# The state update of a linear-attention kernel: one full-array product per head pair, or one 32-column product per head half

## The chip, the core and the metric

The kernel runs on one core of a Trainium2 chip. A core has five engines that run side by side and meet through semaphores: TensorE (PE) for matmuls, VectorE (DVE), ScalarE (ACT), GpSimd (POOL), and SyncE (SP), which here only issues transfers. TensorE reads its operands from SBUF, the 128-partition working memory, and writes to PSUM, the accumulator memory. Weights are loaded by an operation of its own, shown as PEld. The metric is the device time of one execution in microseconds.

## The reference: what is computed

Two blocks follow each other. The first is a linear attention with a decaying state (RWKV-5): 4 batches, 8 heads, 768 positions, head dimension 48. For each position t of a head,

```
y_t   = r_t . (state + (u * k_t) v_t^T)
state = w * state + k_t v_t^T          (w: one decay per head and row, constant in time)
```

The results of all heads, joined to rows of 384, go into a feed-forward block: `silu(x @ w_gate) * (x @ w_val) @ w_out` with inner size 1536, for 3072 rows. All data are fp32; the weights come as 64-bit floats and are rounded to fp32 on the chip.

## The kernel before

**Units.** The sequence is cut into 6 chunks of 128 positions. A unit is one chunk of one batch, all 8 heads; unit i is chunk i // 4 of batch i % 4, so that the state that unit i leaves is read by unit i + 4. There are 24 units. Within a chunk the recurrence is a masked product: `scores` (line 377) makes k times r for each head, a masked copy (line 388, VectorE) puts the upper triangle into the tile `At`, and `outputs` (line 393) multiplies v by `At` and adds the state's share, `Z` times `rT`. The state left by a chunk is `w^128 * (state + khat^T v)`, where `khat` is k scaled so that each position's decay is right.

**Heads in pairs.** Heads 2a and 2a+1 share the partitions: head e of the pair has rows 64e to 64e+47, with rows 48 to 63 empty. `Z[b]` has 128 partitions, 4 pairs and 96 columns, 48 for each head of the pair; only the two blocks in which row head and column head agree may hold anything, the other two must be zero, since y sums over 112 rows of both heads.

**y in column groups.** `outputs` writes 32 partitions of PSUM at a time: four matmuls with 32 weight columns each go to four column groups of TensorE (line 413), and the loop order `for n: for q in range(4)` puts the four groups next to each other.

**The update.** `update(i)` (line 419) takes one matmul per pair over all 112 rows and 96 columns of the pair (line 426), so the products of one head's k with the other head's v are made too. The table `wL` (built once, line 756, from w^128 and the 0/1 table `own`) is zero for them: for the first chunk VectorE multiplies the PSUM result by it into Z (line 437); later VectorE adds the PSUM result to Z (line 439) and GpSimd multiplies Z by the table (line 440). The last chunk has no update, which leaves 20 updates.

**Order of the work.** Every engine runs its queue in program order, and the program is laid out by hand in a loop over steps s (line 803). In step s the unit s+1 is scaled, unit s is turned, scores of unit s-1 and y and update of unit s-2 are made. In between, `gaps(s, n)` hands out pieces of the feed-forward block from the list `todo`, mostly `four` (line 593, sums of products in a scheme that saves multiplications; its matmuls are line 628) and `project` (line 501; line 522). Up to step 11 the gaps also hold the rounding of the weights (`round_act`, `round_dve`, `round_pool`: lines 170 to 207), whose chunks of 768 KB arrive by transfers. From step 12 (`LATE`) y of unit s-2 stands directly behind the scores of unit s-1; before, it stands after the gap 2. The update stands after gap 3 in all of these steps. The first four units are written out ahead of the loop, and their updates too.

**The PSUM ring.** Scores (two tiles), y and update take their tiles from one ring of four, `ps_a`.

**The start.** `make_identity` on GpSimd is followed by 18 matmuls with the identity [...] (line 256, `warm`), then the transposes of unit 0 (line 341), the decay tables on VectorE (lines 272 to 288, `pw`, `pv`), and `own_product`, the u term, on GpSimd (lines 223, 224).

Of the kernel before, what the change touches and what calls it, by code (L numbers as in the profile page):

```python
# [9 lines left out]
FP32 = mybir.dt.float32  # L10
# [3 lines left out]
ALU = mybir.AluOpType  # L14
AX = mybir.AxisListType
P = 128
# [6 lines left out]
def fast(  # L23
# [25 lines left out]
    B, H, S, D = r.shape  # L49
    D2 = 2 * D  # L50
    VW = 2 * D + 16
    HP = H // 2
    R2 = 64 + D
# [5 lines left out]
    cst = ctx.enter_context(tc.tile_pool(name="cst", bufs=1))  # L59
# [4 lines left out]
    ps_a = ctx.enter_context(tc.tile_pool(name="ps_a", bufs=4, space=bass.MemoryType.PSUM))  # L64
# [3 lines left out]
    dve, pool, act, pe, sp = nc.vector, nc.gpsimd, nc.scalar, nc.tensor, nc.sync  # L68
# [3 lines left out]
    ub = cst.tile([P, H, D], FP32, name="ub")  # L72
    kscale = cst.tile([P, H, D], FP32, name="kscale")
    rscale = cst.tile([P, H, D], FP32, name="rscale")
    own = cst.tile([P, 2], FP32, name="own")
    wL = cst.tile([P, HP, 2, D], FP32, name="wL")
    w128 = cst.tile([P, HP], FP32, name="w128")
    bad = cst.tile([P, HP], FP32, name="bad")
    held = cst.tile([P, HP], FP32, name="held")
# [9 lines left out]
    Z = [cst.tile([P, HP, D2], FP32, name=f"Z{b}") for b in range(B)]  # L89
# [29 lines left out]
    def load_v(i):  # L119
        c, b = divmod(i, B)  # L120
        rows = slice(P * c, P * (c + 1))
        for e in range(2):
            sp.dma_start(
                out=v_ld[i % 4][:, :, 64 * e : 64 * e + D],
                in_=v[b, :, rows, :].rearrange("(a e) t d -> e t a d", e=2)[e],
            )
# [82 lines left out]
    def round_weights():  # L209
        if done["act"] > done["pool"]:  # L210
            round_pool()
        round_act()
# [3 lines left out]
    def own_product(i):  # L216
        kl, rl = raw(i)
        if i == 1:

            rk = At[1][:, 0:3, :].rearrange("p x t -> p (x t)").rearrange("p (h d) -> p h d", h=H)  # L220
        else:
            rk = one.tile([P, H, D], FP32, name="rk", tag="rk")[:]
        pool.tensor_mul(rk, rl, kl)
        pool.tensor_mul(rk, rk, ub[:])
        rks[i] = rk

    def own_sum(i):
        dus[i] = three.tile([P, H], FP32, name="du", tag="du")
        dve.tensor_reduce(dus[i][:], rks.pop(i), axis=AX.X, op=ALU.add)
# [4 lines left out]
        dve.memset(t[:, :, D:64], 0.0)  # L234
    dve.memset(hats[:, 0:6, :, D:64], 0.0)
    dve.memset(wcol[:], 1.0)
    for e in range(2):
        sp.dma_start(out=wcol[64 * e : 64 * e + D, :], in_=w.rearrange("(a e) d -> e d a", e=2)[e])
    load(0)
    sp.dma_start(  # L240
        out=ub[:].rearrange("p h d -> p (h d)"),
        in_=bass.AP(tensor=u.tensor, offset=u.offset, ap=[[0, P], [1, H * D]]),
# [9 lines left out]
    def warm(n):  # L252

        ps = ps_f.tile([P, 2, 2 * P], FP32, name="warm", tag="gv")
        for _ in range(n):
            pe.matmul(ps[:, 0, 0:P], ident[:], ident[:], start=True, stop=True)

    warm(18)

    pool.memset(own[:], 1.0)  # L260
    for step, base in ((-64, 0), (64, D - 1)):
        pool.affine_select(
            out=own[:], in_=own[:], compare_op=ALU.is_ge, fill=0.0,
            base=base, pattern=[[step, 2]], channel_multiplier=1 if step < 0 else -1,
        )

    pool.memset(mask[:], 1.0)
    pool.affine_select(
        out=mask[:], in_=mask[:], compare_op=ALU.is_gt, fill=0.0,
        base=0, pattern=[[1, P]], channel_multiplier=-1,  # L270
# [23 lines left out]
    def at(i, a):  # L294

        return HP - 1 - a if i >= BLOCKS and i % 2 == 0 else a
# [14 lines left out]
    def scale(i):  # L311
        scale_k(i)
        scale_r(i)
# [18 lines left out]
    def pair(t, a):  # L332
        return t[:, 2 * a : 2 * a + 2, :].rearrange("p e d -> p (e d)")
# [59 lines left out]
    def outputs(i):  # L393

        c, b = divmod(i, B)
        A, vl, z = At[i % 2], v_ld[i % 4], Z[b]
        rT = turned.pop(i)
        ps = ps_a.tile([P, CC, P], FP32, name="y_ps", tag="a")  # L400
        cols = [[] for _ in range(4)]
        for m in range(4 * CC):
            (cc, q), (a, s) = divmod(m, 4), divmod(m, 3)
            each = [(z[0:R2, a, 32 * s : 32 * s + 32], rT[0:R2, at(i, a), :])] if c > 0 else []
            if s < 2:
                each.append((vl[:, a, 32 * s : 32 * s + 32], A[:, 2 * a, :]))
            if s > 0:
                each.append((vl[:, a, 32 * s + 16 : 32 * s + 48], A[:, 2 * a + 1, :]))
            cols[q] += [(cc, x, n == 0, n == len(each) - 1) for n, x in enumerate(each)]
        for n in range(len(cols[0])):  # L410
            for q in range(4):
                cc, x, start, stop = cols[q][n]
                pe.matmul(  # L413
                    ps[32 * q : 32 * q + 32, cc, :], *x,
                    start=start, stop=stop, skip_group_check=True,
                )
        act.copy(xT[:, i % NX, :, :], ps[:])

    def update(i):
        c, b = divmod(i, B)  # L420
        if c == NCH - 1:
            return
        kh, vl, z = khat[i % 4], v_ld[i % 4], Z[b]
        ps = ps_a.tile([P, HP, D2], FP32, name="u_ps", tag="a")
        for a in range(HP):
            pe.matmul(  # L426
                ps[0:R2, a, :].rearrange("p (e d) -> p e d", e=2),
                pair(kh, a)[:, 0:R2],
                bass.AP(
                    tensor=vl.tensor, offset=vl[:, a, 0:1].offset,  # L430
                    ap=[list(vl[:].ap[0]), [64, 2], [1, D]],
                ),
                start=True, stop=True, skip_group_check=True,
            )
        w = wL[0:R2].rearrange("p a e d -> p a (e d)")
        if c == 0:
            dve.tensor_mul(z[0:R2], ps[0:R2], w)
        else:
            dve.tensor_add(z[0:R2], ps[0:R2], z[0:R2])
            pool.tensor_mul(z[0:R2], z[0:R2], w)  # L440


    hT = {}
# [30 lines left out]
    def weight_sum():  # L474

        n = len(summed)
        o = (wt[1][:], w12, wt[0][:], wt[2][:])[n]
        a, b = ((w22, w12), (w12, w11), (w22, w12), (w21, wt[0][:]))[n]
        pool.tensor_sub(o, a, b)
        summed.append(n)  # L480
# [198 lines left out]
    def feed(n, pops=1):  # L679
        for _ in range(n):  # L680
            ready = [k for k, (need, _) in enumerate(todo) if need <= done["pool"] + len(summed)]
            if ready:
                todo.pop(ready[0])[1]()
            for _ in range(min(pops, len(small))):
                small.popleft()()
# [18 lines left out]
    def gaps(s, n):  # L704

        if s not in EARLY:
            if n == 0:
                share[0] = min(-(-len(todo) // (4 - (s - 9) % 4)), 14)
            feed(share[0] // 5 + (n < share[0] % 5))
            return  # L710
        for what in EARLY[s][n]:
            if what == "R":
                if done["pool"] < NW:
                    round_weights()
                elif len(summed) < 4:
                    weight_sum()
            else:
                feed(1, 3)
# [20 lines left out]
    while small:  # L739
# [13 lines left out]
    outputs(1)  # L753
    round_pool()
    dve.tensor_copy(w128[:].unsqueeze(2), pw[:, :, 0:1])
    dve.tensor_mul(
        wL[:], w128[:].unsqueeze(2).unsqueeze(3).to_broadcast([P, HP, 2, D]),
        own[:].unsqueeze(1).unsqueeze(3).to_broadcast([P, HP, 2, D]),
    )

    dve.tensor_tensor(bad[:], held[:], wcol[:], ALU.not_equal)
    dve.tensor_reduce(badc[:], bad[:], axis=AX.X, op=ALU.add)
# [8 lines left out]
    turn(2)  # L771
    own_product(3)
    update(0)
    update(1)
    own_sum(2)
    diagonal(2)
# [26 lines left out]
    for s in range(4, N + 2):  # L803
        if 4 < s < N:
            own_sum(s)
        if s + 1 < N:
            scale(s + 1)
            own_product(s + 1)
            load_v(s + 1)
            if s + 3 < N:  # L810
                load(s + 3)
        if s < BLOCKS:
            turn(s)
        gaps(s, 0)
        if 4 <= s - 1 < N:
            while small:
                small.popleft()()
            scores(s - 1)
            if s >= LATE:
                outputs(s - 2)  # L820
            gaps(s, 1)
        if BLOCKS <= s < N:
            turn_blocks(s)
        if BLOCKS <= s + 1 < N:
            move_blocks(s + 1)
        gaps(s, 2)
        if s - 2 >= 4 and (s < LATE or s > N):
            outputs(s - 2)
        if s >= 5 and s % 2:
            queue((s - 3) // 2)  # L830
        if s < N:
            diagonal(s)
        if s - 2 >= 4:
            gaps(s, 3)
            update(s - 2)
        gaps(s, 4)
        if s == 12:
            n_ps = ps_a.tile([P, HP, P], FP32, name="n_ps", tag="a")
            pe.matmul(n_ps[0:1, 0, 0:1], badc[:], ones[:], start=True, stop=True)
            act.copy(outside, n_ps[0:1, 0, 0:1])  # L840
# [417 lines left out]
```

## Time and profile before

The median of three runs is 640.49 us (639.94 to 641.51). The profiled execution spans 638.3 us.

| what | number |
|---|---|
| TensorE busy | 624.0 us, 98% of the span |
| VectorE, GpSimd, ScalarE busy | 367.4, 299.1, 242.0 us |
| share of TensorE in the chain that ended last | 85% |
| of it, the update's matmuls (L426) | 2% |
| update: matmul records, mean | 160, 267 ns |
| y: matmul records, mean | 768 of 279 ns and 480 of 276 ns |
| VectorE, add of the update (L439) | 16 of 555 ns |
| GpSimd, product with the table (L440) | 16 of 1056 ns |
| building the table (L756) | 1 of 2186 ns |

How to read it: matmuls overlap each other, so the mean duration of a record is not what it costs; the distance from one start to the next is. Each fp32 matmul of the program appears as two matmul records and two weight loads. A shape such as 128*112 128x96 means 128 rows, 112 weight columns, and 96 streamed columns. The chain of waits goes back from the last instruction to what released it; it says on which engine the end depends at each time.

### The profile page before, as it was taken

The numbers are of one execution on the slowest core, as the hardware profiler recorded it, in microseconds if no ns is written. First come the engines' busy times: TensorE is split into PE (matmuls) and PEld (weight loads), VectorE is DVE, ScalarE is ACT, GpSimd is POOL, SyncE is SP. The second block draws the span as 40 slices with busy tenths as digits, with TensorE's granted clock in tenths as the row PEclk, the third lists the DMA queues.
The fourth block names the chain that finished last, engine by engine and source line by source line (L and its number), as shares of the span: only waits on it lengthen the run. The fifth ranks groups of instructions, "written<-read, shape, count | busy, mean of one in ns | idle before, by whom it ended". The sixth has DMA issues, their size and how long they took to land.

```text
span 638.3 us, 11992 instructions
## 1 busy us (share of the span) xinstructions
PE 624.0 (98%) x4570; PEld 561.6 (88%) x4570; DVE 367.4 (58%) x729; ACT 242.0 (38%) x655; POOL 299.1 (47%) x330
## 2 busy tenths in 40 slices
PE   8889999999999999999999999999999999999996
PEld 8678888899888889988899988889988889988896
DVE  7859998455356565366558255666255545355460
ACT  3558776421343421244431234442243320234310
POOL 5868877934837431754534734631432311444110
PEclk9989999999999999999999999999999999999998
DMA  8969873233322113212221402021100000000001
GB/s 197 263 161 232 223 213 89 40 65 73 79 48 37 33 26 71 66 32 52 45 47 31 109 5 46 16 40 27 51 1 2 1 1 26 26 1 1 2 2 53
DMA packets 138003, 40.40 MB, mean 63 GB/s; under 512 B 128592, under 2 KB 131792, under 8 KB 137936
## 3 DMA queue, kind: packets, MB, share of 16 engines
q1 hardware_dynamic: 134480, 34.82, 24.8%
q10 hardware_dynamic: 3456, 4.72, 2.1%
q8 instruction: 38, 0.62, 0.4%
q14 instruction: 29, 0.24, 0.1%
HBM read 28.51 MB, written 4.72 MB: 52 GB/s over the span
## 4 chain that ended last, share of the span: by engine, by line
PE 85%; DVE 8%; ACT 3%; POOL 1%; issue 1%; DMA 0%; SPq 0%; DVEq 0%; ACTq 0%
PE c_b L628 24%; PE c_a L628 20%; PE o_f L522 13%; PE o_a L522 8%; PE o_b L522 6%; PE y_ps L413 5%; PE gv L451 4%; PE s_ps L383 3%; PE u_ps L426 2%; ACT At L320 1%; DVE wg L196 1%; DVE At L388 1%; DVE wv L196 1%; ACT w_mag L178 1%; DVE wv L197 1%
## 5 line engine op out<-in xcount | busy, mean ns | idle before, releaser
L612 POOL TENSOR_TENSOR hT<-hT,u 128x256 f32<-128x256 f32 x60 | 47.5, 792 | 161.2 <-DVE hT L611 134.2
L635 ACT COPY u<-c_a 128x256 f32<-128x256 f32 x120 | 44.5, 371 | 86.9 <-PE c_a L628 85.6
L628 PE MATMUL c_a<-t,wv 128*128 128x256 f32 x240 | 72.2, 382 | 0.1
L628 PE MATMUL c_b<-xT,wg 128*128 128x256 f32 x240 | 71.7, 380 | 0.0
L608 ACT ACTIVATE sg<-hT 128x256 f32<-128x256 f32 x120 | 50.0, 416 | 54.2 <-DVE hT L637 35.5
L320 ACT ACTIVATE At<-ident,du 128x128 f32<-128x128 f32 x180 | 63.0, 398 | 12.5 <-DVE o_sb L536 7.8
L628 PE MATMUL c_b<-xT,s 128*128 128x256 f32 x240 | 61.6, 379 | 0.0
L642 DVE TENSOR_TENSOR u<-u,c_b 128x256 f32<-128x256 f32 x60 | 25.1, 418 | 62.1 <-PE c_b L628 55.1
L628 PEld LDWEIGHTS c_b<-xT,s 128*128 128x128 f32 x240 | 45.3, 190 | 6.6 <-DVE u L642 0.2
L628 PEld LDWEIGHTS c_a<-t,wv 128*128 128x128 f32 x240 | 44.7, 190 | 7.0 <-ACT u L635 1.1
L628 PEld LDWEIGHTS c_b<-xT,wg 128*128 128x128 f32 x240 | 45.2, 190 | 6.2 <-issue 0.4
L588 POOL TENSOR_TENSOR s<-wv,wg 128x256 f32<-128x256 f32 x24 | 17.8, 741 | 69.8 <-PE o_f L522 55.3
L637 DVE TENSOR_TENSOR hT<-p,c_b 128x256 f32<-128x256 f32 x60 | 25.2, 419 | 43.5 <-PE c_b L628 40.0
L388 DVE COPY_PREDICATED At<-mask,s_ps 128x512 f32<-128x512 int32 x48 | 32.8, 739 | 18.1 <-PE s_ps L383 10.8
L413 PE MATMUL y_ps<-At,v_ld 128*32 128x128 f32 x768 | 36.1, 279 | 4.7 <-DVE At L388 4.7
L451 PE MATMUL gv<-xT,wg 128*128 128x256 f32 x144 | 36.8, 391 | 0.0
L644 DVE TENSOR_TENSOR hT<-u,c_b 128x256 f32<-128x256 f32 x60 | 25.2, 421 | 19.4 <-PE c_b L628 19.2
L413 PEld LDWEIGHTS y_ps<-At,v_ld 128*32 128x32 f32 x768 | 30.9, 112 | 6.1 <-DVE At L388 5.7
L628 PE MATMUL c_b<-t,s 128*128 128x256 f32 x120 | 36.2, 383 | 0.0
L640 DVE TENSOR_TENSOR hT<-hT,c_a 128x256 f32<-128x256 f32 x60 | 25.3, 421 | 18.9 <-PE c_a L628 17.5
L628 PE MATMUL c_b<-xT,wv 128*128 128x256 f32 x120 | 35.9, 381 | 0.0
L628 PE MATMUL c_a<-xT,wg 128*128 128x256 f32 x120 | 35.8, 380 | 0.0
(139 smaller groups left out, 1411.7 us busy)
## 6 DMA issues: line engine op xcount, KB each, us to landing
hats<-hats SPq DMA_DIRECT2D x192, 32.0 KB, 1.9
w_bits<-in_moe_w_gate_dram SPq DMA_DIRECT2D x6, 768.0 KB, 5.9
v_ld<-in_v_dram SPq DMA_DIRECT2D x48, 96.0 KB, 3.0
w_bits<-in_moe_w_val_dram SPq DMA_DIRECT2D x6, 768.0 KB, 5.8
w_bits<-in_moe_w_out_dram SPq DMA_DIRECT2D x6, 768.0 KB, 5.1
out_dram<-o_sb ACTq DMA_DIRECT2D x24, 192.0 KB, 1.9
k_ld<-in_k_dram SPq DMA_DIRECT2D x22, 192.0 KB, 2.8
r_ld<-in_r_dram SPq DMA_DIRECT2D x22, 192.0 KB, 3.7
```

What stands on the lines that cost most here:

```text
L320: lambda h=h: act.activation(At[i % 2][:, h, :], ident[:], AF.Identity, scale=du[:, h : h + 1])
L388: dve.copy_predicated(At[i % 2][:].rearrange("p (a e) t -> p a e t", e=2)[:, :, e], mask[:].bitcast(INT32).unsqueeze(1).to_broadcast([P, H ...
L413: pe.matmul(ps[32 * q : 32 * q + 32, cc, :], *x, start=start, stop=stop, skip_group_check=True,)
L451: pe.matmul(gv[:, o, :].rearrange("p (i t) -> p i t", i=2), wt[:, c, P * f : P * (f + 1)], xT[:, 2 * g % NX : 2 * g % NX + 2, c, :], start ...
L522: pe.matmul(ps, lhs[:, f, :], rhs[:, f, :], start=(f == 0 and n in (0, 1, 4)), stop=(f == FH - 1), skip_group_check=True,)
L608: act.activation(x[what, f][:], h[j], AF.Sigmoid)
L612: pool.tensor_mul(h[1], h[1], x.pop(("u3", f))[:])
L628: pe.matmul(ps.rearrange("p (i t) -> p i t", i=2), lhs, rhs, start=first, stop=what not in ("p2", "p5", "p4", "p3"), skip_group_check=True,)
L635: act.copy(x[nm, f][:], ps)
L637: dve.tensor_add(h[0], x.pop(("p1", f))[:], ps)
L640: dve.tensor_mul(h[0], h[0], ps)
L644: dve.tensor_add(h[1], x.pop(("u2", f))[:], ps)
```

## The change

Each head's share of the state is made by itself. Instead of one product of 112 by 96 per pair there are four products of 32 weight columns and 48 streamed columns, one for each half (32 rows) of each head, each in its own column group of TensorE, as in y. The products of one head with the other are no longer made, so the table that zeroes them, `wL`, and `own` go away. In their place Z is set to zero once at the start, on GpSimd, and the sums and products touch only the blocks of a head: two operations per update, 48 partitions by 192 elements each, with w^128 broadcast along the columns. Last, the update moves from behind gap 3 to directly behind y of the same unit, where the array is already set to 32-column groups.

```diff
-    own = cst.tile([P, 2], FP32, name="own")
-    wL = cst.tile([P, HP, 2, D], FP32, name="wL")
...
     dve.memset(wcol[:], 1.0)
+    for z in Z:
+        pool.memset(z[:], 0.0)
...
     warm(18)
-
-    pool.memset(own[:], 1.0)
-    for step, base in ((-64, 0), (64, D - 1)):
-        pool.affine_select(
-            out=own[:], in_=own[:], compare_op=ALU.is_ge, fill=0.0,
-            base=base, pattern=[[step, 2]], channel_multiplier=1 if step < 0 else -1,
-        )
...
-        ps = ps_a.tile([P, HP, D2], FP32, name="u_ps", tag="a")
+        ps = ps_a.tile([P, HP, D], FP32, name="u_ps", tag="a")
         for a in range(HP):
-            pe.matmul(
-                ps[0:R2, a, :].rearrange("p (e d) -> p e d", e=2),
-                pair(kh, a)[:, 0:R2],
-                bass.AP(
-                    tensor=vl.tensor, offset=vl[:, a, 0:1].offset,
-                    ap=[list(vl[:].ap[0]), [64, 2], [1, D]],
-                ),
-                start=True, stop=True, skip_group_check=True,
-            )
-        w = wL[0:R2].rearrange("p a e d -> p a (e d)")
-        if c == 0:
-            dve.tensor_mul(z[0:R2], ps[0:R2], w)
-        else:
-            dve.tensor_add(z[0:R2], ps[0:R2], z[0:R2])
-            pool.tensor_mul(z[0:R2], z[0:R2], w)
+            for q in range(4):
+                e, half = divmod(q, 2)
+                pe.matmul(
+                    ps[32 * q : 32 * q + 32, a, :], kh[:, 2 * a + e, 32 * half : 32 * half + 32],
+                    vl[:, a, 64 * e : 64 * e + D],
+                    start=True, stop=True, skip_group_check=True,
+                )
+        for e in range(2):
+            rows = slice(64 * e, 64 * e + D)
+            ze = z[rows, :, D * e : D * e + D]
+            w = w128[rows].unsqueeze(2).to_broadcast([D, HP, D])
+            if c == 0:
+                dve.tensor_mul(ze, ps[rows], w)
+            else:
+                dve.tensor_add(ze, ps[rows], ze)
+                pool.tensor_mul(ze, ze, w)
...
     dve.tensor_copy(w128[:].unsqueeze(2), pw[:, :, 0:1])
-    dve.tensor_mul(
-        wL[:], w128[:].unsqueeze(2).unsqueeze(3).to_broadcast([P, HP, 2, D]),
-        own[:].unsqueeze(1).unsqueeze(3).to_broadcast([P, HP, 2, D]),
-    )
...
             if s >= LATE:
                 outputs(s - 2)
+                update(s - 2)
             gaps(s, 1)
...
         if s - 2 >= 4 and (s < LATE or s > N):
             outputs(s - 2)
+            update(s - 2)
...
             gaps(s, 3)
-            update(s - 2)
         gaps(s, 4)
```

## The prediction

> **What bounds the kernel now.** I read the busy shares first, then the slices, then the chain of waits in order of time, then the single matmuls around one update.
>
> ```profile
> PE 624.0 (98%) x4570; PEld 561.6 (88%) x4570; DVE 367.4 (58%) x729; ACT 242.0 (38%) x655; POOL 299.1 (47%) x330
> PE   8889999999999999999999999999999999999996
> ```
>
> TensorE is the bound by share, but the first slices show gaps, so the stages must be parted. The chain in order of time does that:
>
> ```profile
> 21.56 2.19 DVE wL L756
> 23.75 0.89 DVE bad L761
> ...
> 37.55 1.55 PE u_ps L426 x8
> ...
> 98.80 0.48 DVE Z L439
> ...
> 99.33 1.16 PE s_ps L383 x14
> ```
>
> Up to 99.3 us the chain runs mostly over VectorE and ScalarE (rounding of the weights, masks, decay tables), with TensorE on it only from about 36 to 47 us. From 99.3 us to the end it is TensorE almost alone. Busy time by stretch says the same: from 100 to 600 us TensorE is busy for 499.89 of 500 us, VectorE for 269.66, GpSimd for 224.01. So after 99.3 us a TensorE nanosecond saved is a nanosecond of the end, and before it only VectorE's and ScalarE's row counts, with the exception from 36 to 47.
>
> One update in the full stage (start, duration):
>
> ```profile
> 295.90 0.59 PE L628 MATMUL c_b<-xT,wg 128*128 128x256 f32 x2
> 296.34 0.94 PE L426 MATMUL u_ps<-v_ld,hats 128*112 128x96 f32 x8
> 297.11 0.62 PE L628 MATMUL c_a<-t,wv 128*128 128x256 f32 x2
> ```
>
> Each fp32 matmul leaves two records ("passes"): 4 matmuls make x8. From the update's first start to its successor's first start: 297.11 - 296.34 = 0.77 us, or 96 ns a pass. And four rounds of y, whose products are made in 32-column groups:
>
> ```profile
> 308.28 0.28 PE L413 MATMUL y_ps<-rT,Z 112*32 112x128 f32 x1
> 308.29 0.27 PE L413 MATMUL y_ps<-At,v_ld 128*32 128x128 f32 x1
> 308.30 0.37 PE L413 MATMUL y_ps<-rT,Z 112*32 112x128 f32 x3
> 308.40 0.27 PE L413 MATMUL y_ps<-At,v_ld 128*32 128x128 f32 x1
> 308.41 0.28 PE L413 MATMUL y_ps<-rT,Z 112*32 112x128 f32 x2
> 308.50 0.27 PE L413 MATMUL y_ps<-At,v_ld 128*32 128x128 f32 x1
> ```
>
> Passes come four at a time, 6 to 7 ns apart in the trace's full resolution, and the fours come every 0.11 us. So four groups truly run beside each other, and a round of four takes what one pass of 128 columns takes.
>
> [...] after y's last round at about 309.28 the next full matmul starts at 309.49, 0.2 us instead of 0.11, and its second pass comes late too. [...] L756 shows it: 384 elements in 2.19 us, where the same size with one PSUM input takes 0.56 us, beside L207 on GpSimd from 21.51 for 1.82 us.
>
> **The change, part by part.**
>
> *The update's matmuls.* Removed: 8 passes of 112 weight columns, 0.77 us. Added: 16 matmuls, 32 passes, in 4 x 2 = 8 rounds of four groups, each with 32 weight columns and 48 streamed columns. What a round costs is not in the trace, so from both sides. Low: y's 128 columns take 110 ns a round, hence 0.83 ns a column plus 3 to 4 ns; 48 columns then give 40 + 4 = 44 ns [...], 8 x 44 = 0.35 us. High: if what paces y is the issue of its four load-and-matmul pairs and not the stream, a round stays 110 ns and the update takes 0.88 us. I take 44 ns: passes of one round start 7 ns apart, so four pairs can be issued in under 30 ns, and y's rounds fit 128 columns at the same rate as the full matmuls (256 columns in 0.215 us). Saving per update: 0.77 - 0.35 = 0.42 us.
>
> *Its place behind y.* It needs no switch of mode there: y has just set 128x32, and the switch back is paid after y already. Nothing on TensorE waits: the keys were scaled a step and more before, v was used by y, the slot of the PSUM ring was read long ago. The VectorE add now waits for the update right behind the two masked copies. These end at 309.38 in the step shown, the update would end near 309.8, and VectorE's next work before the change came at 310.66 after 1.29 us of idling for TensorE: the add fits there, and I cost it at nothing after 99.3 us. GpSimd's products by w^128 wait for the add; GpSimd is 45% busy there.
>
> *Updates after 99.3 us.* These are units 7 to 19, 13 of them (107.6 to 410.3 us): 13 x 0.42 = 5.5 us off the end. Units 4 to 6 lie where VectorE's chain rules, I count nothing for them.
>
> *Adds and products in halves.* VectorE: one of 384 elements (0.47 us on the chain) becomes two of 192. From 0.42 us for 256 and 0.56 for 384, 192 cost 0.35 each, about 0.28 when they follow one another; +0.1 for each of four adds and +0.2 for the first products of units 0 and 1 on the early chain: +0.6 us before 99.3. GpSimd: 1.06 becomes two of about 0.6, beside other work.
>
> *The start.* Four memsets of Z (384 columns) stand ahead of the identity on GpSimd. A memset of 128 columns took 0.20 us and one of 2 columns 0.10, so 384 take about 0.42, four 1.7 us. The identity releases the 36 warm-up passes (1.42 to 8.1 us) and these stand ahead of the first transposes, which VectorE awaits at 8.83. VectorE was busy until 8.9 anyway, and of the warm-up the slow clock's part may end at the same moment; so +0.8 to +1.6, I take +1.2. The table `own` (0.55 us on GpSimd) sits behind the identity and saves nothing.
>
> *The table wL gone.* VectorE loses 2.19 us on the chain, but the next operation, L761, [...] will wait for the same GpSimd operation that held up L756 until 23.3. So only about 1.2 us comes back.
>
> *Units 2 and 3* at 37.5 and 40.9 us stand on the chain with 1.55 and 1.05 us, at a clock of 0.72. Unit 3's y still has to wait for its masked copy (38.75 at the end), so about 0.3 + 0.6 = 0.9 us is saved.
>
> Sum ahead of 99.3 us: +0.6 + 1.2 - 1.2 - 0.9 = -0.3, between -2 and +1.5. Total: 640.5 - 5.5 - 0.3, about 634.6 us.
>
> **The rivals.** *A, issue paces the groups:* rounds of 110 ns. Updates cost 0.88 for 0.77, +0.11 x 13 = +1.4 us; units 2 and 3 save only 0.3, the start is as above, +0.3 to +0.7: 642.4 us, slower. For it: four load-and-matmul pairs in 110 ns are 27 ns each[...]. Against: the 7 ns. *B, in between:* the feed of instructions holds rounds of 32 passes to some 70 ns (0.56 us an update): 13 x 0.21 = 2.7, so 637.5 us. *C, the gain is lost to waits:* VectorE's add behind y delays the sums that free the banks of c_a and c_b, and TensorE idles 0.4 us a unit: 640 us. For it: those banks are few, and TensorE already waits there now and then (LDWEIGHTS of c_b waits on VectorE's u). Against: VectorE idles after the masked copies. *D, the start goes well:* the warm-up's delay is swallowed and units 4 to 6 count as well: about 632.3 us.
>
> **How the numbers follow.** Forecast 0.62, D 0.10 and B 0.12 (all faster by over 0.3%, that is below 638.6), C 0.08 (same), A 0.08 (slower). The range from 631.8 to 638.4 holds forecast, D and B. Faster 0.83, same 0.08, slower 0.09, with a little of C falling on the slow side.
>
> **What would show it.** Right: the update's x32 passes lie behind y with starts in fours 44 ns apart, and from y's last round to the next full matmul about 0.55 us instead of 0.2; no full-mode u_ps in the gaps; about 13 x 0.42 us fewer between 100 us and the end; L756 gone and L761 longer; the warm-up starting near 3 us. Wrong: fours 100 ns or more apart (A), TensorE idling after y for VectorE (C), or the point at which the chain goes over to TensorE later than 101 us, if the memsets ahead of the identity cost more than I allow.

## The result, and the profile after

The changed kernel takes 630.56 us (median of five, 630.23 to 631.03) against 640.49 us for the kernel before, timed beside it (638.65 to 641.51). The ratio is 0.9845, with a 95% interval of 0.9828 to 0.9863. The profiled spans are 628.5 and 638.3 us, 9.8 us apart. The forecast was 634.6 us with a range down to 631.8: the direction was right, and the gain was larger than the range allowed, 9.9 us instead of 5.9.

The page of the kernel after, first the busy times, then the slices of TensorE, then the shares of the chain that ended last:

```profile
PE 613.8 (98%) x5050; PEld 553.4 (88%) x5050; DVE 364.8 (58%) x748; ACT 242.0 (39%) x655; POOL 299.8 (48%) x347
...
PE   8889999999999999999999999999999999999996
...
PE 83%; DVE 7%; ACT 3%; SPq 2%; DMA 2%; issue 1%; POOL 1%; DVEq 0%; ACTq 0%
```

TensorE made 480 matmul records more and was busy 10.2 us less. It is still the bound. DMA has 2% of the chain; that is new, and comes up again below.

The tile of the update in the kernel after (count, then shortest, median and longest duration in ns, first and last start in us, shape):

```profile
L421 PE MATMUL u_ps<-v_ld,hats x640: 204/206/230, 23.7 to 396.3; 128*32 128x48 f32 x160
L433 DVE TENSOR_TENSOR Z<-u_ps,Z x32: 340/356/362, 67.5 to 397.0; 48x192 f32<-48x192 f32 x32
```

All 640 passes (20 units, 16 matmuls, two passes each) are there, in 32-column groups. In the time order of TensorE of the kernel after (start, duration), one of them lies behind y as planned:

```profile
301.03 0.38 PE L406 MATMUL y_ps<-At,v_ld 128*32 128x128 f32 x5
301.23 0.52 PE L421 MATMUL u_ps<-v_ld,hats 128*32 128x48 f32 x32
301.69 0.70 PE L622 MATMUL c_a<-t,wv 128*128 128x256 f32 x2
```

At the trace's full resolution the starts of this update are these, four to a round:

```
y, last round   301.125 .130 .135 .146
u, first        301.233 .238 .244 .254
u, second       301.275 .280 .287 .296
u, third        301.318 .322 .329 .338
u, fourth       301.360 .364 .372 ...
```

A round every 42 ns, passes 4 to 10 ns apart inside it. From the last pass of y (301.146) to the next full matmul (301.687) it is 0.54 us; in the kernel before, without an update in between, it was 0.20 (309.294 to 309.494). So the update costs 0.34 us of TensorE.

**Where the 9.8 us lie.** Both traces hold the same scores, masked copies and feed-forward matmuls in the same order, so the start of the same operation can be compared. The shift of the scores' starts (after minus before; the times are those of the kernel before):

```
at 11.6  28.3  32.5 | 51.5  58.8 | 72.4  85.0  98.2  112.1 | 124.8 ... 418.5  480.1
 +0.37 -0.11 -0.39 | -2.65 -2.65 | -3.13 -3.59 -4.00 -4.67 | -5.13 ... -9.80  -9.81
```

Three parts: -2.65 us up to 58.8 us (start and units 0 to 3), -2.02 from there to 112.1 us (units 4 to 7, while the weights are rounded), and -5.14 for the 12 units behind it. By its own steps the prediction has -0.7, 0.0 and -5.0 for the same three. The third part is right; the first two hold the error. How far the first can be trusted is seen from the experiments: one pair of traces doesn't fix it.

The chain of waits of the kernel after, in order of time (start, duration), shows what sets the start now:

```profile
17.17 5.87 DMA w_bits<-in_moe_w_gate_dram
...
23.12 0.32 ACT w_mag L176
23.43 6.26 DMA w_bits<-in_moe_w_val_dram
29.72 2.05 DVE wv L194
...
36.72 0.72 DVE At L381
37.45 0.04 issue
37.49 0.90 PE y_ps L406 x25
38.39 0.09 PE u_ps L421 x5
```

Where the chain of before went over VectorE's table (2.19 us at 21.56) and check (0.89), it now goes over two transfers of weights. The two updates that took 1.55 and 1.05 us of the chain near 40 us hardly appear in it.

VectorE of the kernel after, in order of time; the bracket gives the idle time before an operation and what ended it:

```profile
21.59 0.18 DVE L749 COPY w<-tables 128x4 f32<-128x4 f32 x1
21.68 0.15 DVE L751 TENSOR_TENSOR bad<-held,wcol 128x4 f32<-128x4 f32 x1
21.86 0.16 DVE L752 TENSOR_REDUCE badc<-bad 128x1 f32<-128x4 f32 x1
21.97 0.06 DVE L753 MEMSET ones<- 128x1 f32 x1
23.06 0.80 DVE L194 TENSOR_SCALAR wg<-w_bits 128x384 int32<-128x384 int32 x1 [1.03 <-DMA w_bits<-in_moe_w_gate_dram]
```

The check `bad` (L751, before L761) now takes 0.15 us instead of 0.96: it runs before GpSimd's next operation begins (21.75 us). From the copy of w to the end of the check's reduction VectorE had needed 3.48 us (21.34 to 24.82); it now needs 0.43. The 3.0 us are free for the rounding (2.19 of the table, 0.81 of the check), and VectorE then stands 1.03 us for weights that have not arrived.

### The profile page after: what moved, and what is told of

It reads as the page before. It is cut to its first block, busy times and chain, and to the rows that moved or that the text cites. A ratio compares the mean times of both kernels' runs of the same rounds, so it can differ in the third digit from the quotient of the medians.

```text
span 628.5 us, 13043 instructions
## 1 busy us (share of the span) xinstructions
PE 613.8 (98%) x5050; PEld 553.4 (88%) x5050; DVE 364.8 (58%) x748; ACT 242.0 (39%) x655; POOL 299.8 (48%) x347
## 4 chain that ended last, share of the span: by engine, by line
PE 83%; DVE 7%; ACT 3%; SPq 2%; DMA 2%; issue 1%; POOL 1%; DVEq 0%; ACTq 0%
PE c_b L622 25%; PE c_a L622 21%; PE o_f L516 13%; PE o_a L516 8%; PE o_b L516 6%; PE y_ps L406 4%; PE gv L445 4%; PE s_ps L376 3%; DVE wo L194 1%; ACT At L313 1%; DMA w_bits<-in_moe_w_val_dram 1%; DVE wv L194 1%; DMA w_bits<-in_moe_w_gate_dram 1%; DVE wo L195 1%; SPq L115 1%
## 5 line engine op out<-in xcount | busy, mean ns | idle before, releaser
L295 POOL TENSOR_TENSOR hats<-r_ld,rscale 128x384 f32<-128x384 f32 x22 | 23.4, 1065 | 39.5 <-DMA v_ld<-in_v_dram 22.0
```

## The experiments

Shifts below are taken against the trace of the kernel before, as above; a "mark" is the start of one operation there. The trace of the kernel before lies early: six kernels that keep the table have the mark at 13.5 us (a masked copy) 0.2 to 0.9 us later than it. From there to 51.5 us the traces scatter more than that. Four traces are of kernels with the same code up to 51.5 us: the changed kernel and those below with the old place, with full products in units 4 to 6, and with y behind the scores early. They stand at -2.65, -1.54, -1.20 and -0.63 us there. The kernel before and the two that start as it does stand at 0, +0.58 and +0.94. The means are 2.0 us apart, so the -2.65 us of the first part are uncertain by about 1 us. Behind 51.5 us the same code repeats to some hundredths of a us at most steps.

The variants were timed in three later rounds, each beside the kernel before (medians 639.83, 640.11 and 640.59 us), and the changed kernel was not timed again in them. Differences from its 630.56 us are therefore good to some 0.8 us: a variant with an edit that the trace shows to be worth nothing took 631.35.

### What the table and the start are worth

**The table kept.** `own` and `wL` are built as before, and nobody reads them.

```diff
+    own = cst.tile([P, 2], FP32, name="own")
+    wL = cst.tile([P, HP, 2, D], FP32, name="wL")
...
+    pool.memset(own[:], 1.0)
...
+    dve.tensor_mul(
+        wL[:], w128[:].unsqueeze(2).unsqueeze(3).to_broadcast([P, HP, 2, D]),
+        own[:].unsqueeze(1).unsqueeze(3).to_broadcast([P, HP, 2, D]),
+    )
```

> The changed kernel with own and the table wL built again, though nothing reads the table. If the table alone, with the check behind it, held VectorE up (2.8 us in the trace of before, of which some 1.0 us is then lost to waiting for weights), this is 1.3 to 2.0 us slower than the changed kernel: about 632.3 us. If only 1.2 us comes back, as the prediction had it, or if the clock of TensorE at units 2 and 3 made the start faster, 631.8 us or less, with the clock of 36 to 42 us still at 1.

Measured: 633.74 us (0.9905 of before, 0.9890 to 0.9920), 3.2 us more than the changed kernel, and 2.4 and 2.6 us more than two of the variants below that were timed beside it (631.35 and 631.10). Its VectorE, in order of time:

```profile
21.98 2.18 DVE L759 TENSOR_TENSOR wL<-w,own 128x384 f32<-128x384 f32 x1
24.09 0.97 DVE L764 TENSOR_TENSOR bad<-held,wcol 128x4 f32<-128x4 f32 x1
```

Both operations are as long as before the change. So most of the check's 0.96 us belonged to the table: without it, the check slips in ahead of GpSimd. The cost is above both expectations, which points to a second effect.

**Units 0 to 3 as before.** The first four units keep the full product, the table and no zeroing; from unit 4 on all is as in the changed kernel.

```diff
-    for z in Z:
-        pool.memset(z[:], 0.0)
...
+        if c == 0:
+            ps = ps_a.tile([P, HP, D2], FP32, name="u_ps", tag="a")
...
+            w = wL[0:R2].rearrange("p a e d -> p a (e d)")
...
+            return
```

> Changed kernel, but units 0 to 3 update as before, with table wL and without the memsets of Z; units 4 to 19 as changed. If the early gain of 2.65 us lies in the start, this is 2.5 to 3 us slower than the changed kernel, 633.2 us, and the marks of the start lie where those of before do, while units 4 to 6 still each gain about 0.45 us on before. If what was gained at units 4 to 6 came with the start, they gain nothing here and it takes 634.5 us.

Measured: 633.06 us (0.9889, 0.9872 to 0.9905), 2.5 us more than the changed kernel. Its trace stands at +0.57 at 13.1 us and again at 58.8 us, and then gains as the changed kernel does: -1.98 to 112.1 us, -5.12 behind it. So the first part of the gain belongs to the first four units and their preparation, within the scatter of the start.

**The zeroing of Z late.** The four memsets go behind the mask on GpSimd, so the identity is made first.

```diff
-    for z in Z:
-        pool.memset(z[:], 0.0)
...
+    for z in Z:
+        pool.memset(z[:], 0.0)
```

> Changed kernel with the memsets of Z behind the mask on GpSimd, so that the identity comes 1.4 us earlier. In the trace the memsets cost the first transposes only 0.37 us, since the clock came up at the same moment; and from 23 us on the start waits for weights. So 0 to 0.3 us faster: 630.4 us. If the memsets cost what the prediction charged, 1.2 us faster: 629.4 us.

Measured: 631.10 us (0.9867, 0.9849 to 0.9885), against 630.56: no gain is seen. The warm-up starts 1.4 us earlier again, and at the mark of 13.5 us the shift is +0.38 instead of +0.25. In the changed kernel the warm-up starts at 2.84 us and lasts 5.88 us, where it started at 1.42 and lasted 6.93: most of the delay was taken out of its slow first part. There the passes start 213 ns apart, later 112; 26 of the 36 start before the clock comes up at 7.00 us in the kernel before, 16 before it comes up at 6.21 us in the changed kernel.

**The kernel before, TensorE kept awake.** Ten more warm-up matmuls of the identity stand between scores and y of unit 2, where TensorE waits over 2 us.

```diff
     scores(3)
+    warm(10)
     outputs(2)
```

> Kernel before with ten matmuls on the identity between the scores of unit 3 and y of unit 2, where TensorE idled about 2.5 us and its clock then fell to a half from 37.6 to 41.2 us. They add no work on the way. If the fallen clock is part of why the start of before was slow, 1.0 to 1.6 us faster: 639.2 us. If the chain there doesn't run over TensorE, no change, 640.5 us.

Measured: 639.42 us in 20 runs (0.9987, 0.9981 to 0.9994). The reason is in the clock column (PEclk, third from the right) of these stretches. Kernel before:

```profile
core 0: us, PE busy (x) PEld busy (x) DVE busy (x) ACT busy (x) POOL busy (x), PEclk, DMA share, GB/s
36.00:39.00 3.00, 2.80 (x40) 2.19 (x38) 2.52 (x5) 2.08 (x7) 3.00 (x4) 0.79 1.04 246
39.00:42.00 3.00, 3.00 (x42) 2.49 (x42) 0.56 (x1) 0.96 (x3) 1.52 (x2) 0.64 0.30 115
```

Kernel after:

```profile
36.00:39.00 3.00, 2.41 (x104) 1.90 (x92) 1.98 (x5) 1.17 (x5) 2.92 (x4) 1.00 1.07 242
39.00:42.00 3.00, 2.87 (x13) 2.56 (x14) 2.54 (x6) 1.75 (x4) 0.41 (x2) 1.00 0.36 137
```

In the trace of before the clock was at 0.50 for about 3.4 us of these six (from 37.7 us on), in that of after at 1.00; with the ten warm-up matmuls it is 1.00 too, and the mean clock of their 20 runs is 0.9963. The changed kernel's trace has such a stretch as well, at 19.9 to 23.3 us, where VectorE and the transfers rule and no cost is seen. In the first 80 us of all fourteen traces the stretch starts at 19.8 to 21.1 us, at 36.9 to 38.2, at both, or not at all, and it always lasts 3.41 us. The changes of the clock on record stand on a grid of 3.41 us: they are 30.720, 3.413 and 593.919 us apart in the kernel before (9, 1 and 174 times 3.413) and 13.653, 3.413 and 604.159 us in the kernel after (4, 1 and 177 times). So a stretch begins 13.65 us behind the last change or, in the kernel before, 30.72 us. Where the grid lies differs from trace to trace, the clock coming up first at 4.3 to 8.6 us. The whole-run clocks point the same way without a trace: over the 82 runs of the kernel before that were timed beside the experiments, the mean clock is 0.9945; the eight at or below 0.990 take 641.2 us on the mean, the eleven at or above 0.999 take 639.3, and a straight line through all gives 0.16 us for 0.001 of clock. The five runs of the changed kernel have a mean of 0.9982, so by this line about 0.6 us of its gain goes with the clock. That is an estimate, for the runs scatter widely about the line.

**The table kept and TensorE kept awake:** both of these edits on the changed kernel.

> Changed kernel with the table kept (nothing reads it) and ten matmuls on the identity between the scores of unit 3 and y of unit 2. If part of what the table costs is TensorE's clock, which fell to a half after the longer idle, that part, some 0.7 us as in the kernel before, comes back: 633.0 us against 633.7, and the clock from 36 to 42 us is 1. If the clock is of no matter there, 633.7 us.

Measured: 633.03 us (0.9888, 0.9873 to 0.9903), 0.7 us under the first experiment, with the clock at 1.00. So of the 3.2 us there, about 0.7 was clock, and 2.5 is the table with what hangs on it, if the changed kernel's 630.56 is the measure. Against a variant without the table that was timed beside it (631.60, the last experiment) it is 1.4 us. The traces agree with the smaller number: between the marks of 13.5 and 35.1 us, six kernels with the table change by +0.2 us on the mean against before, seven without it by -1.2, a difference of 1.4.

### What the form and the place are worth

These take the change apart in its two ideas. Where the full product stands behind y with adds per head, its cross products are computed and not read.

**Column groups in the old place:** the update of the changed kernel goes back behind gap 3.

```diff
             if s >= LATE:
                 outputs(s - 2)
-                update(s - 2)
...
             gaps(s, 3)
+            update(s - 2)
```

> Changed kernel with the update of units 4 to 19 back behind gap 3, in column groups. Every update then has two switches of mode of its own: 0.09 us in, 0.09 us out and 0.1 us for a late second pass, 0.3 us for 16 units: 630.6 + 4.9 = 635.5 us. If a switch is hidden by the loads that run ahead, 630.6 to 632 us.

Measured: 637.25 us (0.9949, 0.9934 to 0.9964). TensorE of this kernel, in order of time:

```profile
327.23 1.03 PE L622 MATMUL c_b<-xT,s 128*128 128x256 f32 x4
328.18 0.55 PE L421 MATMUL u_ps<-v_ld,hats 128*32 128x48 f32 x32
328.66 4.17 PE L516 MATMUL o_f<-wo,hT 128*128 128x192 f32 x24
```

From start to start at full resolution, it is 0.309 us from the last pass of the full matmuls to the first round instead of the usual 0.216, then 0.342 us for the rounds, then 0.136 us to the next full matmul, whose second pass comes 0.1 us late. The kernel's shift grows by 0.125 us a unit at most steps behind 112 us, that of the changed kernel by 0.46. The way from the full shape into the groups and out again (0.09 us, 0.14 us and the late pass) eats most of what the columns save.

**The full product in the new place:** the kernel before, with only the update moved behind y.

```diff
             if s >= LATE:
                 outputs(s - 2)
+                update(s - 2)
...
             gaps(s, 3)
-            update(s - 2)
```

> Kernel before with the update of units 4 to 19 moved directly behind y, still one full-array product. The switch of mode is paid after y as before; the update lost 0.03 us to a late pass behind it. So no change, 640.0 to 640.5 us. If VectorE's add behind the masked copies makes TensorE wait, slower, 641 us and more; if the earlier release of v and k lets transfers start sooner, up to 1 us faster.

Measured: 641.43 us in 21 runs (1.0016, 1.0008 to 1.0024). Nothing is gained per unit (0.01 us), and it loses 0.7 us between 58.8 and 112.1 us and 0.4 + 0.2 us at two later steps; weight loads for `c_b` wait 0.8 us for VectorE's sums from 200 to 400 us (0.6 at the longest), against 0.4 (0.2) before. The waits of TensorE from 45 to 115 us (who waited for whom, us in total, times, longest):

```profile
PE gv L451 <- DVE hT L459: 1.9, 2, 1.0
PE y_ps L413 <- ACT kT L349: 0.9, 1, 0.9
```

The first line isn't there in the kernel before.

**The changed kernel with the full product:** place, adds per head and zeroing as changed, the product as before.

```diff
-            for q in range(4):
...
+            pe.matmul(
+                ps[0:R2, a, :].rearrange("p (e d) -> p e d", e=2),
+                pair(kh, a)[:, 0:R2],
...
+            cols = slice(D * e, D * e + D)
...
-                dve.tensor_add(ze, ps[rows], ze)
+                dve.tensor_add(ze, ps[rows, :, cols], ze)
```

> Changed kernel with one full-array product per pair in place of the four column groups, for all units; place, adds per head and start as changed. If the form of the product is what saves in the loop, each of 16 units loses 0.45 us and units 2 and 3 about 0.8 us more together: 630.6 + 7.2 + 0.8 = 638.6 us. If the place behind y brings half of the gain, 634.5 us.

Measured: 637.48 us (0.9952, 0.9935 to 0.9969). Behind 112 us the changed kernel is better by 0.47 us a unit. Together with the two above, gains per unit behind 112 us: groups alone 0.125, place alone 0.01, both 0.46. Either idea by itself is worth little; the products in groups need neighbours in groups.

**The full product in units 4 to 6 only,** otherwise the changed kernel.

```diff
+        if 4 <= i <= 6:
+            ps = ps_a.tile([P, HP, D2], FP32, name="u_ps", tag="a")
...
+                    dve.tensor_add(ze, ps[rows, :, cols], ze)
+                    pool.tensor_mul(ze, ze, w)
+            return
```

> Changed kernel, but units 4 to 6 make one full-array product per pair, in the new place, with the adds per head. If TensorE rules there too, each unit costs 0.45 us: 1.35 us slower than the changed kernel, 631.9 us. If VectorE's chain rules there, as the prediction had it, no change: 630.6 us.

Measured: 631.35 us (0.9861, 0.9845 to 0.9878), 0.8 us more. In its trace 1.4 us of lag stand already at 51.5 us, before the first of these updates, where both kernels are the same code, and still 1.4 us at 112.1. So the lag is scatter of the start, and the form of the product in units 4 to 6 is worth nothing.

**Group by group:** the same 16 matmuls, with the four pairs inside and the four groups outside.

```diff
-        for a in range(HP):
-            for q in range(4):
+        for q in range(4):
+            for a in range(HP):
```

> Changed kernel with the 16 products of an update in another order: all four pairs of one column group, then the next group. If the gain comes from four groups running beside each other, the 32 passes now follow one another at 42 to 44 ns: 1.4 us an update for 0.34, 13 updates behind 99 us lose 1.06 us each: 644 to 646 us, slower than before the change. If it comes from short weight loads alone (32 columns for 112), no change: 630.6 us.

Measured: 639.04 us in 20 runs (0.9980, 0.9972 to 0.9988). The update takes 0.92 us instead of 0.34. In this kernel's TensorE:

```profile
306.44 0.40 PE L406 MATMUL y_ps<-At,v_ld 128*32 128x128 f32 x8
306.66 1.10 PE L421 MATMUL u_ps<-v_ld,hats 128*32 128x48 f32 x32
307.69 0.70 PE L622 MATMUL c_a<-t,wv 128*128 128x256 f32 x2
```

So it is the running side by side that saves, not the smaller products as such. I had expected 1.4 us, 32 passes of 42 ns. The starts show why it is less: 306.660 .702 .744 .787 .829 .872 .914 .957 are eight passes 42 ns apart, as many as one group has, and before they are over a second series runs between them, .835 .902 .944 .987 and on. That the second series is the next group, begun before the last had ended, is read from the spacing; the trace does not name the group.

### What the adds per head are worth

**The kernel before behind y, adds per head.** As the place alone, but VectorE's add and GpSimd's product are made per head from unit 4 on (for the first chunk the table is used as before).

```diff
-            dve.tensor_add(z[0:R2], ps[0:R2], z[0:R2])
-            pool.tensor_mul(z[0:R2], z[0:R2], w)
+        for e in range(2):
+            rows = slice(64 * e, 64 * e + D)
...
+            dve.tensor_add(ze, ps[rows, :, cols], ze)
+            pool.tensor_mul(ze, ze, w)
```

> Kernel before with the update directly behind y and its add and product by w^128 made per head (two of 48 by 192), the product of the matmul still one per pair, the table still built and used for the first chunk. If the shape of the adds and products in this place spares VectorE's bit operations some 2 us [...] between 45 and 105 us, those sum to about 20.9 us here (23.7 with whole adds in the same place) and this takes 639.3 us or so, 2 us less than with whole adds. If that difference came with the start of the changed kernel, the same as with whole adds: 641.4 us.

Measured: 639.11 us (0.9974, 0.9964 to 0.9984), 2.3 us under the same kernel with whole adds, which was timed in another round; the two traces are 2.1 us apart. The wait of `gv` for VectorE is gone. The kernels side by side, with the change of the shift from 58.8 to 112.1 us and the durations of the two rounding operations (in us) that follow the add of unit 5:

| kernel | product | place | adds | 58.8 to 112.1 us | two roundings |
|---|---|---|---|---|---|
| before | full | gap 3 | whole | 0 | 0.35 + 2.28 |
| after | groups | y | per head | -2.02 | 0.35 + 1.32 |
| units 4 to 6 full | full in 4 to 6 | y | per head | -2.03 | 0.35 + 1.32 |
| after, full product | full | y | per head | -2.04 | 0.35 + 1.33 |
| before, behind y, per head | full | y | per head | -1.99 | 0.35 + 1.33 |
| groups, old place | groups | gap 3 | per head | -0.11 | 0.38 + 1.92 |
| before, behind y | full | y | whole | +0.72 | 2.41 + 0.50 |

The 2.0 us of this stage come from the place and the adds together, and the product's form has no part in them, not even for unit 7: with full products throughout the stage is as short. What VectorE does with it is seen in its rounding operations (TENSOR_SCALAR, 384 columns). Taken one by one, the 26 of the kernel after from 45 us on differ from those of before by under 0.06 us, but for three: the ones behind the adds of units 4, 5 and 6 are 0.95 to 1.00 us shorter. That is 2.9 us of VectorE, of which 2.0 arrive at 112.1 us. Undisturbed such an operation takes 0.35. VectorE of the kernel before, in one such place:

```profile
84.84 0.55 DVE L439 TENSOR_TENSOR Z<-u_ps,Z 112x384 f32<-112x384 f32 x1
85.30 0.35 DVE L196 TENSOR_SCALAR wo<-w_bits 128x384 int32<-128x384 int32 x1
...
86.23 2.28 DVE L196 TENSOR_SCALAR wo<-w_bits 128x384 int32<-128x384 int32 x1
```

and GpSimd of the kernel before, at the same time:

```profile
85.47 1.04 POOL L440 TENSOR_TENSOR Z<-Z,wL 112x384 f32<-112x384 f32 x1 [3.14 <-DVE Z L439]
86.47 1.82 POOL L207 TENSOR_TENSOR wo<-wo,w_low 128x768 int32<-128x768 int32 x1
```

The rounding of 86.23 begins inside GpSimd's first operation and ends at 88.51, 0.2 us after the second is over. The same place in VectorE of the kernel after:

```profile
80.70 0.73 DVE L433 TENSOR_TENSOR Z<-u_ps,Z 48x192 f32<-48x192 f32 x2
81.46 0.42 DVE L452 TENSOR_TENSOR sg<-sg,gv 128x256 f32<-128x256 f32 x1
...
82.26 0.35 DVE L194 TENSOR_SCALAR wo<-w_bits 128x384 int32<-128x384 int32 x1
...
83.19 1.32 DVE L194 TENSOR_SCALAR wo<-w_bits 128x384 int32<-128x384 int32 x1
```

with GpSimd of the kernel after:

```profile
81.12 1.08 POOL L434 TENSOR_TENSOR Z<-Z,w 48x192 f32<-48x192 f32 x2 [2.15 <-DVE Z L433]
82.28 2.02 POOL L205 TENSOR_TENSOR wo<-wo,w_low 128x768 int32<-128x768 int32 x1
```

Here GpSimd's product lies beside work of VectorE that reads PSUM (`sg` and `hT` from `gv`, 0.40 to 0.42 us each in all 24 places of the trace, so not held up here), and is over when the rounding begins. So the rounding meets one GpSimd operation, not two. That it is held up by them is read from the times: it ends 0.2 us behind GpSimd's rounding in both kernels (84.51 and 84.30 us after, 88.51 and 88.29 before), the same operation takes 0.35, 1.32 or 2.28 us, and GpSimd's rounding takes 2.02 instead of 1.82 where VectorE's began 0.02 us ahead of it. By what the one holds up the other is not shown.

The kernel before behind y with whole adds shows why the adds must be split. Its VectorE:

```profile
84.87 0.55 DVE L439 TENSOR_TENSOR Z<-u_ps,Z 112x384 f32<-112x384 f32 x1
...
86.11 2.41 DVE L196 TENSOR_SCALAR wo<-w_bits 128x384 int32<-128x384 int32 x1
```

and its GpSimd:

```profile
85.49 1.00 POOL L440 TENSOR_TENSOR Z<-Z,wL 112x384 f32<-112x384 f32 x1 [2.35 <-DVE Z L439]
86.45 1.82 POOL L207 TENSOR_TENSOR wo<-wo,w_low 128x768 int32<-128x768 int32 x1
```

Counted from the start of the add, GpSimd's product runs here from 0.62 to 1.62 us, and the rounding starts at 1.25, inside it. With adds per head GpSimd starts behind the first of the two adds and runs from 0.42 to 1.50 us, while VectorE, busy longer with two adds, comes to the rounding only at 1.56. These times are the same within 0.02 us at all three places, in all four kernels of the table with adds per head behind y. In the old place the product of the adds per head is over in time too, but there the second rounding starts 0.14 to 0.21 us behind the start of GpSimd's rounding and waits for nearly all of it. That the order of starts decides is read from the traces; no experiment moves it alone. In the changed kernel the margin is 0.06 us.

### A further try

**y behind the scores from step 7 on:** in the changed kernel y and the update stand directly behind the scores only from step 12.

```diff
-    LATE = 12
+    LATE = 7
```

> Changed kernel with y and update of units 5 to 9 directly behind the scores too, which spares TensorE one way out of a tiling mode and one way in, 0.2 us a step. TensorE rules only from unit 7 on: 0.4 to 0.6 us faster, 630.0 us. If the add behind the masked copies makes TensorE wait where VectorE is busiest, up to 1.5 us slower.

Measured: 631.60 us (0.9860, 0.9845 to 0.9875). Not faster. Its trace lies 2.0 us behind that of the changed kernel already at 51.5 us, before the first unit that was moved; from there to the last scores both gain the same (7.2 us). Two steps gain 0.2 us more each, as expected, and the same amount is lost elsewhere; TensorE waits 1.5 us for ScalarE's keys and 0.9 for VectorE between 45 and 115 us, against 0.9 and 0.6 in the changed kernel. No version tried beat the changed kernel.

## Why the prediction was right in direction and wrong in size

**Right: the update's matmuls.** 0.34 us were measured for the 0.35 forecast, rounds of 42 ns for 44. It rested on the 7 ns between passes of different groups in y, here 4 to 10 ns, and on 0.83 ns a column plus 3 to 4 ns, taken from y's 110 ns for 128 columns, here 42 ns for 48, and both held; rivals A (rounds of 110 ns) and B (70 ns) are out. A pass can be shorter still: both passes of the matmul `n_ps`, with a single column, start 26 ns apart, which is less than the 42 ns of a round. Per unit the gain is 0.46 and not 0.42, since the old update also made its successor's second pass 0.03 us late. Two of the later steps gain only 0.25 and 0.28, so that the 12 units behind 112 us bring 5.14 us where 12 x 0.42 = 5.04 was forecast. That the two are so near is in part luck, since the larger gain per unit and the two poor steps cancel.

**Right: the place behind y costs no switch, and the add there costs next to nothing after 99.3 us.** The update's first round starts 0.087 us behind the last pass of y, as a round of y behind the one before it (0.086 to 0.093), and from its last pass to the next full matmul it is 0.14 us. In the old place the same rounds lose 0.33 us a unit. Rival C's wait for VectorE is there, but small: every kernel with the full product behind y loses 0.4 + 0.2 us at the same two steps, with whole adds or with adds per head, and in the changed kernel it is at most the 0.4 us that its two poor steps miss.

**Right: "Units 4 to 6 lie where VectorE's chain rules, I count nothing for them", as far as the matmuls go.** The experiment with the full product in these units shows it. It holds for unit 7 as well, which the prediction counted on TensorE with 0.42 us: in the changed kernel its update, at 100.2 us, still lies where VectorE rules. Rival D came nearest with 632.3 us and one of its two reasons was wrong: it let these units count on TensorE.

**Wrong, the largest: "Adds and products in halves ... +0.6 us before 99.3".** The step that failed is this price: each operation was charged by its size alone, and GpSimd's products were put at nothing, as lying "beside other work". In this stage VectorE's time is set by how long its rounding lasts beside GpSimd's operations, up to 2.28 us for the 0.35 us it takes alone, and the new order of adds and products shortened that by 2.9 us. From 58.8 to 112.1 us my sum has +0.4 for four adds and -0.4 for unit 7, which makes 0.0; the trace has -2.02. The prediction saw `wL` take 2.19 us beside GpSimd and did not ask which other operations lie so.

**Wrong: "The start ... +0.8 to +1.6, I take +1.2".** Kernels that zero Z first have the mark at 13.5 us about 0.2 us later on the mean than kernels that don't (0.71 against 0.47, with single traces from 0.2 to 1.6 and from 0 to 0.9), and the late zeroing gained nothing. The prediction named what hides it, that the slow part of the warm-up ends at the same moment (7.00 us before, 6.21 after), and then took the middle of its bounds. This term is too large by about 1.0 us.

**Wrong in size: "So only about 1.2 us comes back" for the table.** The step was that the check "will wait for the same GpSimd operation". It doesn't wait; it starts 0.07 us ahead of it (21.68 and 21.75 us). So 3.0 us of VectorE come free, part of which the late weights take again (1.03 us of idling). What arrives at the end is 1.4 us by the means of the traces and by the kernels timed side by side, and up to 2.5 us against the changed kernel's own time.

**Units 2 and 3: forecast 0.9 us.** From 37.4 to 51.5 us the groups bring 1.0 and 0.6 us in the two traces in which the clock falls, and 1.3 where it stays up; the clock alone, in the kernel before, brings 1.2. With the clock kept up by extra matmuls, the full product has 1.2 us there and the groups 1.3, so the two gains do not add: most of what the groups save here they save only because the clock is low. The step itself was good for the clock of 0.72 that it named, and that the clock could come up was not in my sum. What keeps it up can be read in part. All five traces with the full product in units 2 and 3 and no extra matmuls fall there, after TensorE had stood idle for 1.6 to 2.2 us. Of the seven with groups, three have their grid where no trace falls in the first 80 us (the clock first up at 7.7, 8.2 or 8.6 us); one of these had idled 2.1 us. Of the other four, the two that idled 2.1 and 2.2 us fall, and the two that idled 1.3 and 1.4 us don't. So the place of the grid and the length of the pause sort all twelve; that they are the cause is not shown with so few.

The sum ahead of 112 us was -0.7 in the forecast's terms and is -4.7 in the two traces, some 4 if the start is taken from means; the range for it, down to -2, covered the unknown size of the zeroing and of the table, but not VectorE's roundings beside GpSimd. (The forecast's own terms add up to 634.7 us, not 634.6; nothing hangs on it.)

## What to carry to other kernels

Products in column groups pay where their neighbours are in column groups too: here form alone gave 0.125 us, place alone nothing, both 0.46. Where a vector engine rules a stage, look first at how far the same operation's duration spreads; if it spreads by a factor of six, as here from 0.35 to 2.28 us, the order of the other engine's work is worth more than the operations' sizes, and an edit that moves a small operation brought 2.0 us here, or cost 0.7. One trace of each kernel does not size a gain in a start that waits for transfers: the same code stood up to 2 us apart. When an operation goes away, redo the waits of what stood behind it, up to the next thing that limits, which here was a transfer.

## What the runs showed of the hardware

- A pass of 48 columns in one group takes 42 ns, and four groups beside each other take 42 ns together, between 10 and 11 ns a pass; across groups the passes of a round start 4 to 10 ns apart. The time a column is 0.88 ns for 48 columns and 0.86 for y's 128. The two one-column passes of `n_ps` start 26 ns apart in the traces of both kernels.
- With the groups issued one after the other, 32 passes start within 0.90 us, 29 ns each on the mean, where passes of one group are 42 ns apart.
- A visit to the 32-column groups between full matmuls cost 0.09 us on the way in (0.309 for 0.216), 0.14 us from the last round to the next full matmul, and left the second pass of that matmul 0.1 us late.
- Four memsets of 128 x 384 on GpSimd took 1.48 us, 0.42 for each and 0.35 from start to start. All but about 0.2 us of it hid behind a warm-up whose slow part ended by the clock and not by the number of its matmuls: the clock came up at 7.00 us behind 26 slow passes in the kernel before, at 6.21 us behind 16 in the kernel after, and over the fourteen traces at 4.3 to 8.6 us, behind 14 to 27.
- The changes of TensorE's clock lay 9, 1 and 174 times 3.413 us apart in the kernel before and 4, 1 and 177 times in the kernel after; the first of them came at 7.00 and 6.21 us. A stretch at half clock followed a pause of 1.6 us in one trace, and none followed a pause of 2.1 us in another.
- The same VectorE rounding (384 columns of int32) took 0.35 us where GpSimd stood idle (at 83.12 us in the kernel before), and behind the add of unit 5 it took 1.32 us where it met the rest of one and 2.28 us where it met the rest of one and a whole second.
